# Two weights asked for in two pieces each, and a new order of every engine's work

## The chip, the cores and the metric

The kernel runs on one core of a Trainium2 chip. The time is the device time of one execution in microseconds. Before the change the median of three runs is 166.47 us (165.52 to 167.43). The profile is of one further execution, recorded by the hardware profiler, with its own time.

## The reference

Two stages, one behind the other. The first is a linear attention with a decay and a bonus (RWKV-5), for 4 batches, 8 heads, 768 steps and a head size of 48:

```
for t in range(S):
    kt, vt, rt = (k[:, :, t], v[:, :, t], r[:, :, t])
    cur = np.einsum('bhd,bhe->bhde', u[None] * kt, vt)
    y[:, :, t] = np.einsum('bhd,bhde->bhe', rt, state + cur)
    state = w[None, :, :, None] * state + np.einsum('bhd,bhe->bhde', kt, vt)
```

The second is an MLP mixer on x, the heads of y side by side (4 x 768 x 384):

```
xt = x.transpose(0, 2, 1)
h = np.maximum(xt @ w_tok1, 0.0) @ w_tok2       # 768 -> 256 -> 768, along the tokens
u = x + h.transpose(0, 2, 1)
h2 = np.maximum(u @ w_ch1, 0.0) @ w_ch2         # 384 -> 1536 -> 384, along the channels
return (u + h2).astype(np.float32)
```

## The kernel before, in words

**Units.** The sequence of each batch is cut into 6 chunks of 128 steps, so there are 24 units, numbered 0 to 23; unit u belongs to batch u // 6. For each unit SP loads three tiles k, r and v (128 x 384 f32, 192 KB each; `load`, L742). `kp` and `rp` multiply k and r by powers of the decay, on VectorE or POOL. `trk` and `trr` transpose them on TensorE (from unit 14 on a DMA does), `rk` copies them out, `at` makes the scores inside the chunk, `AT` masks them (for some halves `raw` copies first), `vb` casts v on ScalarE, `kv` adds k times v to the running state in PSUM, `S` copies the state out, `pg` and `yd` make the bonus term, `yS` and `y` add up the unit's output, and `x` writes it as bf16. Unit 3 adds its bonus by a matmul in f32 (`yi3`).

**Mixer.** When the six x of a batch are there, `hid` (six pairs of matmuls with w_tok1) makes the hidden layer of the tokens, `hr` the relu, and `bk` (or `ux` and `ub`, for the first half of batch 0, directly transposed) multiplies by w_tok2. `us` adds x, `tu` and `uT` transpose, `z` makes the channels' hidden layer in 12 pieces of 128 (j = 0 to 11) for each half of the batch, `zr` its relu, `h` the product with w_ch2 in four quarters, `os` adds u, and SP stores.

**Weights.** POOL asks for the weights by DMA, cast to bf16 on the way (`weight`, L753): w0 is w_tok1, w1 is w_tok2, w2 and w4 are the two halves of w_ch1, w3 and w5 those of w_ch2. Each stands in POOL's queue between products; the queue is served in order.

**What sets the order.** Each engine's work is written out by name in `ORDER` (L508). `graph` (L181) builds all steps with what they wait for and with costs; `Plan.run` replays `ORDER` with these costs, and the program is emitted in the order of the starts found. The costs and the `wafter` table (after which step a weight is asked for) shape only this replay, that is, how the engines' instructions are interleaved in the program and where `fill` puts small idle matmuls (27 of them before, all ahead of the first `z`). On the chip each engine takes its own instructions in order, and waits are on what an instruction reads or overwrites. The load of k of unit 6 is held until y5 is done, so that weights go first. SP, at most eight loads in flight, issues loads in `ORDER`'s succession.

All instructions go through one helper, so the profile has them under its line, L617; tiles tell them apart: `ld_k`, `ld_r`, `ld_v` the loads, `kpr` the products, `tr_ps` the transposes, `at_ps` the scores, `y_ps` the output, `h_ps` both `hid` and `h`, `z_ps` the channels' hidden layer, `hT_ps` and `ut_ps` the product with w_tok2, `wtok` and `wch` the weights, `osb` the result.

Of the kernel before, what the change touches and what calls it, by code (L numbers as in the profile page):

```python
# [21 lines left out]
B, H, S, D = 4, 8, 768, 48  # L22
T = 128
C = S // T
G = C // 2
HP = H // 2
NJ = 12
# [146 lines left out]
MM = 0.165  # L174
# [6 lines left out]
def graph(do, cfg):  # L181
# [39 lines left out]
    def weight(i, after):  # L221
        wi[i] = s = p.add(f"i:w{i}", [("POOL", 0.9, cfg.get("wseen", 1.0), True)], after, rank=-50, emit=do("weight", i))
        took = cfg.get("wtime", (3.0, 2.6, 3.1, 7.7, 3.1) if 5 not in cfg["wafter"] else (3.0, 2.6, 3.1, 3.9, 3.1, 3.9))[i]
        wx[i] = p.transfer(f"x:w{i}", s, took, took + 1.0, -1.0)
# [123 lines left out]
    for b in range(B):  # L348
# [20 lines left out]
        for sg in range(2):  # L369
            if (b, sg) in direct:  # L370
                last = C * (b + 1) - 1
                for mm in range(3):
# [4 lines left out]
                    t = p.add(f"ub{n}", [("PE", 2 * MM + 0.01, 2 * MM + 0.14)], [t, wx[1]] + (hr if mm else first), rank=r - 0.2 + 0.01 * mm, emit=do("ub", b, sg, mm))  # L377
# [5 lines left out]
            for c in range(sg * G, sg * G + G):  # L383
                n = 3 if (b, c) in cfg.get("xpe", ()) else 2
                bk = p.add(f"bk{b}_{c}", [("PE", n * MM + 0.01 * (b > 0), n * MM + 0.13 + 0.01 * (b > 0))], hr + [wx[1]], take=True, rank=r + 0.01 * c, emit=do("bk", b, c))
# [10 lines left out]
        for sg in range(2):  # L396
            zr = []
            for j in range(NJ):
                old = downs[2 * b + sg - 3] if 2 * b + sg >= 3 else []
                if j == 0:  # L400
                    z0, z_before = None, z0
                z = p.add(f"z{b}_{sg}_{j}", [("PE", 3 * MM, 3 * MM + 0.13)], [z_before if j == 0 else z0] + old + uT[3 * sg:3 * sg + 3] + [wx[2] if j < NJ // 2 else wx[4]], take=True, rank=m + 0.1 * sg + 0.001 * j, emit=do("z", b, sg, j))
                z0 = z if j == 0 else z0
                ways = [ACT1, DVEP + (False, 0.3)] if b in cfg.get("zr_dve", range(B)) else [ACT1]
                zr.append(p.add(f"zr{b}_{sg}_{j}", ways, [z], give=[f"z{b}_{sg}_{j}"], rank=o, emit=do("zr", b, sg, j)))
            downs.append([])
            for si in range(3):
# [3 lines left out]
                for part in range(parts):  # L411
                    h, n, mm = None, f"{b}_{c}" + "ab"[part] * (parts > 1), MM / parts + (0.005 if parts > 1 else 0.0)
                    for q in range(4):
                        x = 3 * mm + (own if q == 0 else 0.0)
                        h = p.add(f"h{n}_{q}", [("PE", x, x + 0.13)], zr[3 * q:3 * q + 3] + [wx[3] if q < 2 else wx.get(5, wx[3]), h], take=(q == 0), rank=m + 0.1 * sg + 0.05 + 0.01 * si + 0.001 * part - (0.02 if q else 0), emit=do("h", b, c, q, part, parts))
# [22 lines left out]
    for s in p.steps:  # L438
# [41 lines left out]
    + [('w', 0), ('w', 1), ('w', 2), ('w', 4), ('w', 3), ('w', 5)],  # L480
    wafter={0: 'x:r4', 1: 'kp5', 2: 'rp5', 4: 'rp5', 3: 'rp5', 5: 'rp5'},
    slack={'v5': 0.9},
# [4 lines left out]
    wtime=(3.0, 2.6, 3.1, 5.2, 3.1, 3.9),  # L487
# [13 lines left out]
    half=8.3,  # L501
# [41 lines left out]
    ),  # L543
    "ACT": (
# [558 lines left out]
```

## Time and profile before

| | us |
|---|---|
| median of three runs | 166.47 |
| the profiled execution | 165.6 |
| its span, from the first to the last instruction | 163.9 |
| TensorE busy | 154.8 |
| VectorE busy | 119.7 |
| ScalarE busy | 74.0 |
| POOL busy | 59.1 |

The page shows busy time by engine, 40 slices of the span (a digit is the busy share in tenths), and the chain of work that ended last, followed back from the end. Matmuls overlap in the array, so the busy time of TensorE is not work at its peak. A row of the timeline has start, length, engine, line, operation, output<-inputs and count, and in brackets the idle time before it with what ended it. A row of the stretches has the busy time and count of each engine in its window, then the granted clock of TensorE, the share of the DMA engines and GB/s. A landing is counted from the start of the issuing instruction.

### The profile page before, as it was taken

What the parts mean: (1) busy time and instruction counts of PE and PEld (TensorE: products, weight loads), DVE (VectorE), ACT (ScalarE), POOL (GpSimd) and SP (SyncE); (2) the same over time, 40 slices, a digit from 0 to 9 for tenths busy, and PEclk for the clock granted to TensorE, in tenths of its full rate; (3) what the DMA queues carried; (4) which work ended last, traced back from release to release, by engine and by line L of the source; (5) the groups of instructions that cost most, each with busy time, mean ns of one, the idle gap of its engine ahead of it and who ended that gap; (6) DMA issues with size and microseconds to landing.
All of it is one profiled execution on the core that took longest, in us unless ns stands there. A gap on an engine that the chain in (4) does not pass through costs nothing.

```text
span 163.9 us, 3809 instructions
## 1 busy us (share of the span) xinstructions
PE 154.8 (94%) x1487; PEld 99.2 (61%) x1487; DVE 119.7 (73%) x254; ACT 74.0 (45%) x160; POOL 59.1 (36%) x74
## 2 busy tenths in 40 slices
PE   6988799999999999999999999999999999999990
PEld 3476565656576767665666565666566666655670
DVE  5679878547089998896998989999999665223330
ACT  4899671552389635588504420445134102621400
POOL 7157860000055495954459542182702000000000
PEclk9999789999999999999999999999999999999997
DMA  5999999999999998999499999999934032501212
GB/s 106 222 212 219 152 201 201 185 184 198 199 221 237 210 233 168 214 159 208 99 167 206 226 212 150 236 234 151 204 67 145 0 72 43 177 0 48 96 48 98
DMA packets 97427, 26.26 MB, mean 160 GB/s; under 512 B 90753, under 2 KB 97410, under 8 KB 97410
## 3 DMA queue, kind: packets, MB, share of 16 engines
q1 hardware_dynamic: 93920, 22.88, 69.9%
q0 software_dynamic: 3488, 3.15, 12.1%
q8 instruction: 11, 0.18, 0.4%
q14 instruction: 6, 0.05, 0.1%
q10 hardware_dynamic: 2, 0.00, 0.0%
HBM read 20.65 MB, written 4.72 MB: 155 GB/s over the span
## 4 chain that ended last, share of the span: by engine, by line
PE 84%; SPq 7%; DMA 3%; ACT 3%; issue 1%; DVE 0%; ACTq 0%
PE h_ps L617 34%; PE z_ps L617 29%; SPq L617 7%; PE y_ps L617 6%; PE at_ps L617 5%; PE hT_ps L617 4%; DMA ld_v<-in_v_dram 3%; PE tr_ps L617 3%; PE kv_ps L617 3%; ACT rk L617 1%; PE t_ps L617 1%; ACT raw L617 0%; ACT vb L617 0%; PE ut_ps L617 0%; ACT S L617 0%
## 5 line engine op out<-in xcount | busy, mean ns | idle before, releaser
L617 PE MATMUL h_ps<-wch,zr 128*128 128x384 bf16 (+1 forms) x300 | 55.2, 320 | 0.0
L617 PE MATMUL z_ps<-uT,wch 128*128 128x384 bf16 x288 | 53.9, 326 | 0.1
L617 ACT ACTIVATE zr<-z_ps 128x384 bf16<-128x384 f32 x66 | 30.8, 492 | 50.7 <-PE z_ps L617 50.2
L617 PEld LDWEIGHTS <-zr 128*128 128x128 bf16 x300 | 27.4, 98 | 15.2
L617 PEld LDWEIGHTS <-wch 128*128 128x128 bf16 x288 | 26.6, 98 | 16.2 <-issue 0.2
L617 DVE TENSOR_TENSOR AT<-at_ps,mask 128x512 bf16<-128x512 f32 x43 | 28.9, 684 | 1.5 <-PE at_ps L617 1.2
L617 DVE TENSOR_SCALAR zr<-z_ps 128x384 bf16<-128x384 f32 x30 | 15.9, 553 | 11.7 <-PE z_ps L617 11.2
L617 POOL TENSOR_TENSOR kpr<-ld_r,wp 128x384 bf16<-128x384 f32 x14 | 14.6, 1044 | 24.9 <-DVE pr L617 22.2
L617 POOL TENSOR_TENSOR kpr<-ld_k,wn 128x384 bf16<-128x384 f32 x16 | 16.3, 1019 | 10.0 <-DMA ld_k<-in_k_dram 5.8
L617 DVE TENSOR_TENSOR osb<-u_sb,h_ps 128x384 f32<-128x384 bf16 (+1 forms) x22 | 11.7, 532 | 11.0 <-PE h_ps L617 11.0
L617 ACT COPY rk<-tr_ps 128x512 bf16<-128x512 bf16 (+1 forms) x23 | 15.1, 682 | 8.9 <-PE tr_ps L617 8.8
L617 PEld LDWEIGHTS <-rk 48*128 48x128 bf16 (+1 forms) x272 | 11.0, 97 | 8.7 <-issue 4.6
L617 PEld LDWEIGHTS <-kpr 128*128 128x128 bf16 x192 | 12.5, 101 | 5.2 <-issue 1.6
L617 POOL TENSOR_TENSOR yd<-vb,adg 128x384 f32<-128x384 bf16 x12 | 10.3, 858 | 12.0 <-ACT vb L617 8.3
L617 DVE TENSOR_TENSOR x_b<-y_ps,yd 128x384 bf16<-128x384 f32 x23 | 12.6, 552 | 2.1 <-PE y_ps L617 1.9
L617 ACT CAST vb<-ld_v 128x384 bf16<-128x384 f32 x24 | 12.2, 514 | 3.4 <-DMA ld_v<-in_v_dram 3.3
L617 DVE TENSOR_TENSOR u_sb<-x_b,hT_ps 128x384 bf16<-128x384 bf16 x21 | 11.2, 549 | 2.3 <-PE hT_ps L617 1.9
L617 PE MATMUL tr_ps<-ident,kpr 128*128 128x128 bf16 x112 | 10.7, 233 | 1.0 <-ACT rk L617 0.6
L617 PEld LDWEIGHTS <-wtok 128*128 128x128 bf16 x90 | 8.1, 97 | 4.8 <-issue 0.4
L617 PE MATMUL at_ps<-rk 48*128 48x128 bf16 x192 | 9.8, 222 | 1.2 <-ACT rk L617 0.4
L617 DVE TENSOR_TENSOR pr<-tr_ps,rk 128x512 bf16<-128x512 bf16 x14 | 5.9, 419 | 5.9 <-ACT rk L617 5.8
L617 PE MATMUL h_ps<-x_b,wtok 128*128 128x384 bf16 x48 | 10.0, 325 | 0.0
(87 smaller groups left out, 157.5 us busy)
## 6 DMA issues: line engine op xcount, KB each, us to landing
ld_k<-in_k_dram SPq DMA_DIRECT2D x24, 192.0 KB, 3.8
ld_r<-in_r_dram SPq DMA_DIRECT2D x24, 192.0 KB, 3.9
ld_v<-in_v_dram SPq DMA_DIRECT2D x24, 192.0 KB, 3.8
out_dram<-osb SPq DMA_DIRECT2D x23, 192.0 KB, 2.3
wch<-in_moe_w_ch_dram POOLq DMA_DIRECT2D x4, 576.0 KB, 12.2
wtok<-in_moe_w_tok_dram POOLq DMA_DIRECT2D x2, 384.0 KB, 5.4
u_bc<-in_u_dram SPq DMA_DIRECT2D x1, 192.0 KB, 4.4
out_dram<-osb SPq DMA_DIRECT2D x2, 96.0 KB, 2.6
```

The lines of the kernel that those rows point to most:

```text
L617: ins = tc.keep_in_program_order(f(*args, **kw))
```

## The change

Three things. w1 is split by columns into w1 (the first 384) and w6 (the others), w2 into w2 (the first 256 columns, j = 0 and 1) and w7 (the next 512, j = 2 to 5), so there are eight weight transfers in place of six; products wait for the piece that they read. In the planner w0 is asked for after the transfer of v of unit 4 in place of r of unit 4, w1 and w2 after that of r of unit 5, and the times of the transfers are other numbers. And the order of all five engines is new.

```diff
-                    t = p.add(f"ub{n}", [("PE", 2 * MM + 0.01, 2 * MM + 0.14)], [t, wx[1]] + (hr if mm else first), rank=r - 0.2 + 0.01 * mm, emit=do("ub", b, sg, mm))
+                    t = p.add(f"ub{n}", [("PE", 2 * MM + 0.01, 2 * MM + 0.14)], [t, wx[1 if sg == 0 else 6]] + (hr if mm else first), rank=r - 0.2 + 0.01 * mm, emit=do("ub", b, sg, mm))
...
-    + [('w', 0), ('w', 1), ('w', 2), ('w', 4), ('w', 3), ('w', 5)],
-    wafter={0: 'x:r4', 1: 'kp5', 2: 'rp5', 4: 'rp5', 3: 'rp5', 5: 'rp5'},
-    slack={'v5': 0.9},
+    + [('w', 0), ('w', 1), ('w', 2), ('w', 6), ('w', 7), ('w', 4), ('w', 3), ('w', 5)],
+    wafter={0: 'x:v4', 1: 'x:r5', 2: 'x:r5', 6: 'rp5', 7: 'rp5', 4: 'rp5', 3: 'rp5', 5: 'rp5'},
+    slack={'v5': 0.6},
...
-    wtime=(3.0, 2.6, 3.1, 5.2, 3.1, 3.9),
+    wtime={0: 3.0, 1: 1.4, 2: 1.15, 6: 1.4, 7: 2.1, 3: 5.2, 4: 3.1, 5: 3.9},
...
-    half=8.3,
+    half=9.0,
...
-        t, src = [(wtok1, moe_w_tok1), (wtok2, moe_w_tok2), (wch1, moe_w_ch1), (wch2, moe_w_ch2), (wch1, moe_w_ch1), (wch2, moe_w_ch2)][i]
-        cols = {2: slice(0, dch // 2), 4: slice(dch // 2, dch)}.get(i, slice(None))
-        rows = {3: slice(0, NJ // 2), 5: slice(NJ // 2, NJ)}.get(i, slice(None)) if 5 in CFG["wafter"] else slice(None)
+        t, src, rows, cols = {
+            0: (wtok1, moe_w_tok1, slice(None), slice(None)),
+            1: (wtok2, moe_w_tok2, slice(None), slice(0, G * T)),
+            6: (wtok2, moe_w_tok2, slice(None), slice(G * T, S)),
+            2: (wch1, moe_w_ch1, slice(None), slice(0, 2 * 128)),
+            7: (wch1, moe_w_ch1, slice(None), slice(2 * 128, dch // 2)),
+            4: (wch1, moe_w_ch1, slice(None), slice(dch // 2, dch)),
+            3: (wch2, moe_w_ch2, slice(0, NJ // 2), slice(None)),
+            5: (wch2, moe_w_ch2, slice(NJ // 2, NJ), slice(None)),
+        }[i]
```

The head of the new order, as far as it is spoken of below (before, then after):

```diff
 SP
-i:k1 i:r2 i:k0 i:r0 i:r1 i:v0 i:k2 i:v1 i:k3 i:r3 i:v2 i:k4 i:r4 i:k5 i:v3 i:r5 i:v4 i:v5 i:k6 i:r6 i:k7 i:r7 i:v6
+i:r0 i:k1 i:k0 i:k2 i:r1 i:r2 i:r3 i:v0 i:k3 i:v1 i:v2 i:r4 i:k4 i:v4 i:v6 i:k5 i:r5 i:v5 i:v3 i:r6 i:k6 i:r7 i:k7
 POOL
-kp2 kp3 rp3 kp4 rp4 i:w0 kp5 rp5 i:w1 i:w2 i:w4 i:w3 i:w5 rp8
+rp1 kp3 rp3 kp4 rp4 i:w0 kp5 i:w1 rp5 i:w2 i:w6 i:w7 i:w4 i:w3 i:w5 kp6 kp7 rp8
 ACT
-vb2 rk3 wGm vb3 rk4 S3 vb4 rk5 x3 S4 raw5 vb5 hr0_1a
+wGm S1 vb2 rk3 rk4 vb4 vb3 S3 rk5 vb5 x3 raw5 S4 hr0_0a
 DVE
-S2 yd2 AT1_3 pr4 yd3 AT1_4 AT0_4 x2 pr5 AT0_5 AT1_5 yd5 yd4 x4 x5 hr0_0a
+S2 yd2 pr3 AT1_3 AT0_3 pr4 AT1_4 yd3 x2 AT0_4 yd4 pr5 AT0_5 yd5 AT1_5 x4 x5 hr0_1a
 PE
-trk4 at3 pg3 trr4 kv3 y2 trk5 at4 yS3 trr5 yi3 y3 kv4 pg4 at5 yS5 pg5 ux0_0_1 yS4 y4 y5 hid0_0 hid0_1 hid0_2 hid0_3 hid0_4 hid0_5 ux0_0_2
+trk4 yS2 y2 trr4 at3 trk5 at4 pg4 pg3 yS3 kv3 trr5 yi3 kv4 y3 at5 yS4 y4 pg5 hid0_0 hid0_1 hid0_2 yS5 y5 hid0_3 hid0_4 ux0_0_0 hid0_5 ux0_0_1
```

The program after has 40 of the idle matmuls in place of 27; its other matmuls are the same. In the whole order, DVE has 230 steps in place of 237, ScalarE 150 in place of 152, POOL 69 in place of 58.

More of the change, by code (lines that the diff above doesn't have):

```diff
@@ L222, in weight @@
         wi[i] = s = p.add(f"i:w{i}", [("POOL", 0.9, cfg.get("wseen", 1.0), True)], after, rank=-50, emit=do("weight", i))
-        took = cfg.get("wtime", (3.0, 2.6, 3.1, 7.7, 3.1) if 5 not in cfg["wafter"] else (3.0, 2.6, 3.1, 3.9, 3.1, 3.9))[i]
+        took = cfg["wtime"][i]
         wx[i] = p.transfer(f"x:w{i}", s, took, took + 1.0, -1.0)
@@ L384, in graph @@
                 n = 3 if (b, c) in cfg.get("xpe", ()) else 2
-                bk = p.add(f"bk{b}_{c}", [("PE", n * MM + 0.01 * (b > 0), n * MM + 0.13 + 0.01 * (b > 0))], hr + [wx[1]], take=True, rank=r + 0.01 * c, emit=do("bk", b, c))
+                bk = p.add(f"bk{b}_{c}", [("PE", n * MM + 0.01 * (b > 0), n * MM + 0.13 + 0.01 * (b > 0))], hr + [wx[1 if c < G else 6]], take=True, rank=r + 0.01 * c, emit=do("bk", b, c))
                 us = p.add(f"us{b}_{c}", [ACT1, DVEP] if n == 3 else [DVEP], [bk], give=[f"bk{b}_{c}"], rank=r, emit=do("us", b, c))
@@ L401, in graph @@
                     z0, z_before = None, z0
-                z = p.add(f"z{b}_{sg}_{j}", [("PE", 3 * MM, 3 * MM + 0.13)], [z_before if j == 0 else z0] + old + uT[3 * sg:3 * sg + 3] + [wx[2] if j < NJ // 2 else wx[4]], take=True, rank=m + 0.1 * sg + 0.001 * j, emit=do("z", b, sg, j))
+                z = p.add(f"z{b}_{sg}_{j}", [("PE", 3 * MM, 3 * MM + 0.13)], [z_before if j == 0 else z0] + old + uT[3 * sg:3 * sg + 3] + [wx[2 if j < 2 else 7 if j < NJ // 2 else 4]], take=True, rank=m + 0.1 * sg + 0.001 * j, emit=do("z", b, sg, j))
                 z0 = z if j == 0 else z0
@@ L414, in graph @@
                         x = 3 * mm + (own if q == 0 else 0.0)
-                        h = p.add(f"h{n}_{q}", [("PE", x, x + 0.13)], zr[3 * q:3 * q + 3] + [wx[3] if q < 2 else wx.get(5, wx[3]), h], take=(q == 0), rank=m + 0.1 * sg + 0.05 + 0.01 * si + 0.001 * part - (0.02 if q else 0), emit=do("h", b, c, q, part, parts))
+                        h = p.add(f"h{n}_{q}", [("PE", x, x + 0.13)], zr[3 * q:3 * q + 3] + [wx[3 if q < 2 else 5], h], take=(q == 0), rank=m + 0.1 * sg + 0.05 + 0.01 * si + 0.001 * part - (0.02 if q else 0), emit=do("h", b, c, q, part, parts))
                     ways = [ACT1, DVEP] if (b, sg) in direct else [DVEP]
@@ L531 @@
     "DVE": (
[11 rows of a table removed]
[11 rows of a table added]
     ),
     "ACT": (
[8 rows of a table removed]
[8 rows of a table added]
     ),
     "POOL": (
-        "kp2 kp3 rp3 kp4 rp4 i:w0 kp5 rp5 i:w1 i:w2 i:w4 i:w3 i:w5 rp8 kp8 kp9 kp10 yd7 yd8 rp11 yd9 rp12 kp12 yd10 yd11 rp13 kp13 yd12 "
-        "kp14 rp14 rp16 ku14 ku15 ku16 kp16 yd14 rku16 yd16 ku18 rku18 yd15 kp19 rp18 kp18 rp19 yd17 rku19 kp20 rp21 rku20 rp22 kp21 yd19 "
-        "kp23 ku23 rku22 rp23 yd23 "
[3 rows of a table added]
     ),
     "SP": (
[5 rows of a table removed]
[5 rows of a table added]
         "i:o3_3 i:o3_4 i:o3_5a i:o3_5b "
```

89 rows, old and new, of the table ORDER are left out of this document.

## The prediction

> **What bounds the kernel now.** I read the page first, then the chain in order of time, the stretches, and the head's timeline engine by engine.
>
> ```profile
> span 163.9 us, 3809 instructions
> PE 154.8 (94%) x1487; PEld 99.2 (61%) x1487; DVE 119.7 (73%) x254; ACT 74.0 (45%) x160; POOL 59.1 (36%) x74
> PE   6988799999999999999999999999999999999990
> PEclk9999789999999999999999999999999999999997
> PE 84%; SPq 7%; DMA 3%; ACT 3%; issue 1%; DVE 0%; ACTq 0%
> 29.88:42.74 12.86, 12.86 (x88) 8.00 (x88) 6.36 (x14) 4.88 (x10) 0.00 (x0) 1.00 1.15 187
> 42.74:155.00 112.26, 111.62 (x1072) 70.74 (x1071) 88.73 (x178) 48.54 (x107) 43.45 (x45) 1.00 0.78 157
> ```
>
> The columns after the length are TensorE, weight loads, VectorE, ScalarE and POOL, then the clock. TensorE is dense: from 29.88 to 42.74 us it is never idle, from 42.74 to 155 for 112.26 - 111.62 = 0.64 us. Its digits below 9 lie in the first five slices of 4.1 us. What is left to win or lose lies there; a start of the dense part that moves by some time moves the end by the same, because no stall behind it is large enough to take it up. There the chain runs through the loads:
>
> ```profile
> 12.83 4.69 DMA ld_v<-in_v_dram
> 17.54 0.51 ACT vb L617
> 18.05 0.92 ACT rk L617
> ...
> 24.23 0.57 PE y_ps L617 x20
> 24.80 2.19 PE h_ps L617 x12
> ```
>
> The load that lands at 17.52 is v of unit 3, the 15th that SP asks for. Units 4 and 5 hang behind it, then the six hidden products of batch 0 (hid0), whose last pair starts at about 26.5:
>
> ```profile
> 24.64 2.34 PE L617 MATMUL h_ps<-x_b,wtok 128*128 128x384 bf16 x12
> 27.21 0.50 PE L617 MATMUL at_ps<-wtok,h1r 128*128 128x384 bf16 x2
> 29.88 1.14 PE L617 MATMUL z_ps<-uT,wch 128*128 128x384 bf16 x6
> ```
>
> (26.98 is the end of the group; two matmuls pass from the start of the last pair, 0.16 and 0.33 us.)
>
> **The change part by part.** *Weights in two pieces.* Two more issues on POOL; the weights' issues take 0.77 to 0.89 us.
>
> ```profile
> 13.79 1.00 POOL L617 TENSOR_TENSOR kpr<-ld_k,wn 128x384 bf16<-128x384 f32 x1 [0.81 <-DMA ld_k<-in_k_dram]
> 14.90 1.00 POOL L617 TENSOR_TENSOR kpr<-ld_r,wp 128x384 bf16<-128x384 f32 x1
> 15.85 0.89 POOL L617 DMA_DIRECT2D wtok<-in_moe_w_tok_dram  x1
> 19.25 0.77 POOL L617 DMA_DIRECT2D wtok<-in_moe_w_tok_dram  x1
> 20.02 3.19 POOL L617 DMA_DIRECT2D wch<-in_moe_w_ch_dram  x4
> DMA to landing us min/median/max: 5.2/5.2/5.2
> DMA to landing us min/median/max: 8.3/8.3/8.3
> ```
>
> The second token weight lands at 19.25 + 5.2 = 24.4 and is first read at 27.2; the first up weight lands at 20.02 + 8.3 = 28.3 and is read at 29.88. Neither ends a wait that the chain shows, so having their first halves earlier is worth 0 us while hid0 comes no earlier than now. The 1.6 us of POOL push rp5 back by one issue (0.8); trr5, its reader, stands behind kv3 on TensorE and waits longer for that anyway (below). If the cover were gone, it would cost that 0.8. The Trainium skill ("DMA: Bandwidth & Descriptors", section on the anatomy of one DMA on the GpSimd path) gives each such DMA a fixed 2.0 us, which speaks against pieces: two more would, as an estimate from the page, be 4 us if nothing hid them. No landing here decides it, but four issues 0.8 us apart kept the queue full, so I do not count it.
>
> *First weight behind v of unit 4.* In the program no wait for v4 stands on it: `i:w0` follows `rp4` on POOL, before and after. What moves it is k4, which SP now asks for as 13th load, not 12th. Loads go out at (16.51 - 0.81) / 17 = 0.92 us each (first and 18th issue, rows below), so kp4, rp4 and w0 come about 0.9 to 1.0 later: w0 at 16.8.
>
> *The new succession of loads* decides the case. SP now asks in the order ... r4 k4 v4 v6 k5 r5 v5 v3 r6: v3 goes from 15th to 19th, with v of unit 6, whose products on TensorE stand behind trk6 (40 us), ahead of it. The 18th load before is v5:
>
> ```profile
> 0.81 0.45 SPq L617 DMA_DIRECT2D ld_k<-in_k_dram  x1
> ...
> L617 SPq DMA_DIRECT2D ld_v<-in_v_dram x2: 937/1368/1798, 14.7 to 16.5; - x2
> ...
> DMA to landing us min/median/max: 5.0/5.3/5.7
> ...
> DMA to landing us min/median/max: 3.3/3.9/5.9
> ...
> q0 software_dynamic: 525, 0.27, 134.1%
> q1 hardware_dynamic: 30, 0.00, 2.3%
> ```
>
> The first two rows are v4's and v5's issue (ns, shortest to longest; v5 at 16.51) and landing, the third is that of all v loads up to 60 us. v5 took 5.7 us against 3.9 in the median, landing at 22.2. The last two rows (18.75 to 20.25 us) say why: w0's packets had the engines almost to themselves. After the change one more load and w0 still stand ahead of v3, and w0 moves by the same 0.9 to 1.0 as v3's issue, so v3 meets w0 as v5 did: V = 22.2 + 0.92 = 23.1. Were w0 not later at all, the same 19 loads and w0 would still have to pass: again 23.1. Bounds: 19.9 (no contention) and 23.9 (w1's first piece beside it too, half of its 1.6 us).
>
> *What waits for V.* On TensorE kv3 stands ahead of trr5, yi3, kv4, y3, at5, yS4, y4 and hid0; on ScalarE vb3 ahead of S3, rk5, vb5, x3, raw5 and S4; on VectorE yd3 ahead of x2, AT0_4, yd4 and pr5. All this piles up behind one load and is then run off in order, mostly at ScalarE's pace:
>
> ```profile
> 18.86 0.63 ACT L617 CAST S<-kv_ps 48x192 bf16<-48x192 f32 x2
> 20.52 1.01 ACT L617 COPY rk<-tr_ps 128x1024 bf16<-128x1024 bf16 x1 [0.35 <-PE tr_ps L617]
> 22.23 0.48 ACT L617 CAST x_b<-y_ps 128x384 bf16<-128x384 f32 x1 [0.69 <-PE y_ps L617]
> 23.27 0.58 ACT L617 CAST raw<-at_ps 128x512 bf16<-128x512 f32 x1
> 18.27 0.36 PE L617 MATMUL y_ps<-vb,AT 128*128 128x48 bf16 x8
> 23.29 0.33 PE L617 MATMUL y_ps<-S,rk 128*128 128x96 bf16 x4
> L617 DVE TENSOR_TENSOR x_b<-y_ps,yd 128x384 bf16<-128x384 f32 x23 | 12.6, 552 | 2.1 <-PE y_ps L617 1.9
> ```
>
> From V: vb3 0.53, kv3 0.4, S3 0.63, rk5 1.0, vb5 0.5, x3 0.5, raw5 0.6, S4 0.6 make 4.75; yS5 and y5 0.55; x5 0.55; then hid0_5, the last pair, at V + 5.9 = 29.0. hid0_0 to hid0_2 and hid0_4 lie beside it; TensorE has nothing else, as its queue is in order.
>
> *The clock.* The trace shows a stretch at half clock:
>
> ```profile
> 15.28:18.69 3.41, 2.20 (x41) 1.45 (x38) 3.14 (x7) 2.42 (x6) 2.84 (x4) 1.00 0.85 153
> 18.69:22.10 3.41, 3.29 (x32) 2.10 (x29) 2.98 (x6) 2.32 (x5) 3.41 (x5) 0.50 1.31 197
> 20.28 1.59 PE L617 MATMUL y_ps<-yd,ident_w 128*128 128x384 f32 x2
> ```
>
> A stretch of 3.41 us with 2.20 us of work was followed by one at 0.50, and that one, 3.29 busy, by full clock. After the change TensorE has less than 2 us of work between 19 and 23 (trk5, at4, pg4, pg3, yS3), so half clock should last into the run-off: yi3 takes its 1.59 again (about 0.8 at full clock, an estimate from its half) and hid0_0 to hid0_2, six matmuls of 0.16, twice their 1.0. Between 0 (all hidden by ScalarE) and 1.8 (0.8 and 1.0 in full) I take 0.6, since raw5 and S4 hide part. The Trainium skill ("TensorE: Matmul & The Clock Gate", Part 1) says that the clock falls after at least one idle window of about 3.4 us; the row's window was busy for 64%, so it differs from the page, and I go by the row. By the page the term would be 0, and the sum 0.6 less.
>
> *Everything behind.* The order of units 6 to 23 changes on every engine, trk6 comes nine products earlier, and nine products more stand on POOL (1.0 us each) and seven steps fewer on VectorE (0.55). TensorE's matmuls are the same but for 40 fillers in place of 27, all ahead of hid0. The cover is TensorE's density, with 0.64 us idle in 112: an order can win at most that 0.64, and one late tile costs about as much (-0.6 to +1.0; I take 0, between them). k6 is held until y5, which comes 3 us later than now, and it took long to land beside the weights:
>
> ```profile
> DMA to landing us min/median/max: 10.7/10.7/10.7
> ```
>
> Asked for at 28.5 it would land at 39.2, and kp6 be done at 40.3 on POOL; trk6, behind 16 products of 0.49 us, stands at about 33 + 8 = 41, so it is just in time.
>
> *Sum.* hid0_5 at 23.1 + 5.9 + 0.6 = 29.6 instead of 26.5: +3.1; three products of ux0 now stand ahead of it, -0.2. So +2.9. The profiled execution took 165.6 us (span 163.9 and 1.7 around it): 168.5. The median of the runs shown is 166.47, 0.9 above it; 169.4 from there. I take 169.0, between.
>
> **The rivals.** *v3 slips in ahead of w0* (no change). The issue of the 17th load took 1.80 us before, twice the usual, and only thereby came v5 behind w0. Without that, v3 is asked for 0.9 us sooner, at 16.6, and lands 3.9 later at 20.5, its warm run-off ends at 26.4, less 0.2: 165.6 - 0.3 = 165.3, or 165.8 between the two frames. Against it: w0 is only one load's time later. *The same and the clock kept* (the other side: faster). If v3 lands by 19.9 (16.6 and 3.3, the shortest of the v loads), TensorE's pause is too short to lose the clock, hid0_5 comes at 25.8, and the later 0.64 of stalls goes too: -0.7 - 0.2 - 0.6 = -1.5, 164.1, or 164.6. It decides from V = 20.2 on downwards. For it: the stretch at half clock, which makes yi3 alone take 1.59 where about 0.8 would do. Against it: v6 takes 0.92 us ahead of v3. *Half clock reaches into the dense part* (slower still). Stretches of 3.41 us end at 25.5, 28.9 and 32.3; if the run-off doesn't fill the one up to 28.9, the 2.7 us from 29.6 to 32.3 do half their work, +1.4: 170.4. *The change does not do what it says*: w0 has no wait for v4; this leaves the sum as it is, shown above.
>
> **How the numbers follow.** Forecast (169.0) 0.50, half clock further 0.15, v3 ahead of w0 0.22, and that with the clock kept 0.13. A measurement tells about 1% from no change here: 164.8 to 168.1. So faster 0.13, same 0.22, slower 0.65. The range leaves out most of the faster case and the top of the slowest: 165.3 to 171.0. The forecast's own range is 167.6 to 170.0.
>
> **What would show it.** In the profile after: v3's landing near 23 us, a wait of ScalarE's vb for ld_v of 3 us or more, hardly any TensorE work from 20 to 23, a half clock that lasts beyond 22.1, hid0's last pair near 29.6 and the first z product near 33 (29.88 before), then 130 us to the end of TensorE as before. w0 issued near 16.8. It would be wrong if v3 landed by 21, if vb3's followers ran faster than ScalarE's order lets them, or if TensorE's idle time behind 42 us grew or shrank by more than 1 us.

## The result and the profile after

The changed kernel takes 170.62 us (median of four executions, 169.83 to 170.93) against 166.0 before (median of four): a ratio of 1.031, with an interval of 1.026 to 1.036, so it is slower by about 3%. The profiled execution took 169.83 us with a span of 167.8, against 165.6 and 163.9: +4.2 and +3.9. The forecast was 169.0 us, an increase of 1.5% over the 166.47 us that stood for the kernel before and of 1.8% over 166.0: the direction and the place were right, the size was too small. (A ratio here is of undisturbed executions alone and can differ from the quotient of the medians: single executions of the kernel before scatter from 165.7 to 171.9 us in the experiments' sessions, and a quarter to somewhat over half of those are left out, as are six of ten with v6 behind v3, four of ten with the pieces alone, two of four with whole weights and three of four with whole weights on the same plan.)

The page of the kernel after, the same rows as before; the last is ScalarE's `vb`, with its idle time and what ended it:

```profile
span 167.8 us, 3843 instructions
PE 154.9 (92%) x1500; PEld 99.5 (59%) x1500; DVE 116.6 (70%) x247; ACT 71.8 (43%) x158; POOL 67.9 (40%) x85
PE   6978609999999989999999999999999999999991
PEclk9999956999999999999999999999999999999999
PE 81%; SPq 9%; DMA 4%; ACT 2%; DVE 1%; issue 1%
L617 ACT CAST vb<-ld_v 128x384 bf16<-128x384 f32 x24 | 12.0, 513 | 5.7 <-DMA ld_v<-in_v_dram 5.7
```

TensorE is busy for as long as before (154.8), so the 3.9 us are idle time, and the digits put it into one slice, the sixth: a 0 between 21.0 and 25.2 us. Behind that slice the row is as dense as it was. All that VectorE and ScalarE were relieved of (3.1 and 2.2 us) does not show in the time.

The chain of work that ended last, after, from the load of v of unit 3 on (start, length, what):

```profile
17.54 6.73 DMA ld_v<-in_v_dram
24.29 0.52 ACT vb L617
24.85 0.48 PE kv_ps L617 x4
25.33 0.43 PE tr_ps L617 x4
25.76 1.39 PE y_ps L617 x2
...
30.99 0.17 PE at_ps L617 x3
31.15 0.33 PE h_ps L617 x2
```

v of unit 3 (v3) lands at 24.27 us instead of 17.52, and from `kv` of unit 3 on every link is TensorE's, up to the last pair of hidden products (hid0_5). By TensorE's timeline that pair starts at 30.99 instead of 26.5; its link in the chain begins only where the link before it ends. The stretches show TensorE's pause, the clock, and the dense part from the first z product to the start of the last matmul (TensorE, weight loads, VectorE, ScalarE, POOL, clock, DMA share, GB/s). After:

```profile
17.83:21.24 3.41, 1.73 (x32) 1.12 (x30) 2.03 (x4) 0.78 (x2) 2.70 (x4) 1.00 1.02 138
21.24:24.65 3.41, 0.00 (x0) 0.00 (x0) 0.00 (x0) 0.36 (x1) 3.41 (x6) 0.50 1.31 205
24.65:28.07 3.42, 3.22 (x28) 2.23 (x29) 2.51 (x5) 2.45 (x6) 1.29 (x2) 0.50 1.33 202
28.07:31.48 3.41, 3.41 (x54) 2.52 (x51) 2.52 (x5) 1.46 (x5) 0.00 (x0) 1.00 1.19 211
24.85:30.99 6.14, 6.14 (x73) 4.39 (x73) 5.01 (x10) 3.63 (x8) 1.09 (x2) 0.74 1.27 207
34.15:164.15 130.00, 129.06 (x1200) 82.41 (x1197) 93.87 (x188) 50.81 (x114) 50.78 (x54) 1.00 0.74 150
```

And the same dense part before:

```profile
29.88:159.67 129.79, 129.15 (x1196) 82.18 (x1196) 96.56 (x195) 53.42 (x117) 43.45 (x45) 1.00 0.79 156
```

The dense part starts 4.27 us later and lasts 130.00 us instead of 129.79. What follows, to the end of the span, is 0.6 us shorter (3.6 us, 4.2 before). 4.27 + 0.21 - 0.6 = 3.9: that is the whole difference of the spans.

Why the load took 6.73 us shows in what the DMA engines moved between its issue and its landing: packets, then by queue (q1 the loads, q0 the weights; the last figure of a row is the share of the engines' time). Before, for v of unit 5, the load on which the forecast was built (16.5 to 22.25 us; the first row has the engines' busy tenths in 40 slices of that window):

```profile
DMA  6200279999559999999999999999999999989899
DMA packets 3183, 0.98 MB, mean 170 GB/s; under 512 B 2316, under 2 KB 3183, under 8 KB 3183
q0 software_dynamic: 883, 0.55, 69.2%
q1 hardware_dynamic: 2300, 0.43, 39.8%
```

After, for v3 (17.55 to 24.3 us):

```profile
DMA packets 4484, 1.17 MB, mean 173 GB/s; under 512 B 3585, under 2 KB 4484, under 8 KB 4484
q1 hardware_dynamic: 3569, 0.68, 63.6%
q0 software_dynamic: 915, 0.49, 51.9%
...
q0 software_dynamic: 582, 0.30, 86.4%
q1 hardware_dynamic: 581, 0.11, 41.6%
```

The rate is the same, 170 and 173 GB/s; what differs is the amount. The weights' packets are about as many, but 1269 more of the loads' passed. Not all of these stood ahead of v3. The loads' packets from the start of the span, up to the landing of v5 before and up to that of v3 after:

```profile
q1 hardware_dynamic: 18720, 3.54, 82.3%
...
q1 hardware_dynamic: 20360, 3.85, 84.1%
```

The first count is 18 loads of 1040 packets and nothing more, as the load behind v5 is the held k6. The second is 19 loads (19760 packets) and 600 packets of a twentieth: r6, which the new succession puts between v3 and the held k6, and which SP asked for at 18.24. So of the 1269 packets about 670, two thirds of a load, stood ahead of v3, and 600 belong to the load behind it and passed beside it. Both queues together moved 0.19 MB more. At 173 GB/s that is 1.1 us, and the landing took 6.73 - 5.72 = 1.01 us longer. How much of it r6 costs is not shown: no run holds back r6 alone.

The last two rows of the view of after are from 19.5 to 22.0 us: weights and loads go packet by packet, 582 to 581. The Trainium skill ("DMA: Bandwidth & Descriptors", the paragraph on arbitration under queues, rings and completion order) says that each DMA engine takes the queues in turn, a packet at a time. Equal counts agree with it; the 525 to 30 of the kernel before, quoted in the prediction, do not look like turns.

### The profile page after: what moved, and what is told of

Its sections match the earlier page's. It is cut to its first block, busy times and chain, and to the rows that moved or that the text cites. A ratio compares the mean times of both kernels' runs of the same rounds, so it can differ in the third digit from the quotient of the medians.

```text
span 167.8 us, 3843 instructions
## 1 busy us (share of the span) xinstructions
PE 154.9 (92%) x1500; PEld 99.5 (59%) x1500; DVE 116.6 (70%) x247; ACT 71.8 (43%) x158; POOL 67.9 (40%) x85
## 4 chain that ended last, share of the span: by engine, by line
PE 81%; SPq 9%; DMA 4%; ACT 2%; DVE 1%; issue 1%
PE h_ps L617 33%; PE z_ps L617 28%; SPq L617 9%; PE y_ps L617 5%; PE at_ps L617 4%; DMA ld_v<-in_v_dram 4%; PE hT_ps L617 3%; PE kv_ps L617 3%; PE tr_ps L617 2%; PE t_ps L617 1%; ACT rk L617 1%; DVE S L617 0%; ACT vb L617 0%; PE ut_ps L617 0%; ACT osb L617 0%
## 5 line engine op out<-in xcount | busy, mean ns | idle before, releaser
L617 ACT ACTIVATE zr<-z_ps 128x384 bf16<-128x384 f32 x65 | 29.9, 490 | 54.4 <-PE z_ps L617 53.7
L617 PEld LDWEIGHTS <-zr 128*128 128x128 bf16 x300 | 27.5, 98 | 15.5
L617 DVE TENSOR_TENSOR AT<-at_ps,mask 128x512 bf16<-128x512 f32 x43 | 28.4, 683 | 4.4 <-PE at_ps L617 4.4
L617 POOL TENSOR_TENSOR kpr<-ld_k,wn 128x384 bf16<-128x384 f32 x17 | 17.1, 1009 | 26.2 <-DMA ld_k<-in_k_dram 19.2
L617 DVE TENSOR_SCALAR zr<-z_ps 128x384 bf16<-128x384 f32 x31 | 16.6, 553 | 8.1 <-PE z_ps L617 7.0
L617 POOL TENSOR_TENSOR yd<-vb,adg 128x384 f32<-128x384 bf16 x16 | 13.2, 829 | 18.6 <-ACT vb L617 7.8
L617 POOL TENSOR_TENSOR kpr<-ld_r,wp 128x384 bf16<-128x384 f32 x15 | 15.9, 1062 | 11.8 <-DVE x_b L617 6.3
L617 DVE TENSOR_TENSOR u_sb<-x_b,hT_ps 128x384 bf16<-128x384 bf16 x21 | 10.7, 549 | 2.9 <-PE hT_ps L617 2.8
L617 PE MATMUL kv_ps<-vb,kpr 128*128 128x96 bf16 x80 | 7.0, 213 | 4.7 <-ACT vb L617 4.7
```

What stands on the lines that cost most here:

```text
L617: ins = tc.keep_in_program_order(f(*args, **kw))
```

## The experiments

Theory A: the place of v3 in SP's succession is the whole cost; all engines wait for it, and nothing behind takes up or adds time. Rivals: the pieces cost time (B), the new order of the other engines costs time (C), the weights' packets, not the place, make v3 late (D), and half clock is the larger part (E).

### v3 early: its place alone undone

The changed kernel with v3 and v6 exchanged in SP's order.

```diff
-i:v2 i:r4 i:k4 i:v4 i:v6 i:k5 i:r5 i:v5 i:v3 i:r6 i:k6
+i:v2 i:r4 i:k4 i:v4 i:v3 i:k5 i:r5 i:v5 i:v6 i:r6 i:k6
```

> The changed kernel with one swap in SP's succession of loads: v3 and v6 change places (r4 k4 v4 v3 k5 r5 v5 v6 r6), nothing else in any engine's order. If the late v3 is what costs (theory): v3 lands at about 17.1 to 17.6 us, where v6 did, the run-off behind it is over before v5 comes, and v5, still landing near 23.6, becomes the last: vb5, x3, raw5, S4, yS5, y5, x5 behind it give hid0's last pair at about 27.0 in place of 31.0; time about 166 us, level with the kernel before (ratio 0.99 to 1.01). If the new order of units 6 to 23 or the pieces of the weights cost (rivals): it stays within 1 us of the changed kernel, 169.5 us or more.

Measured: 166.89 us, a ratio to the kernel before of 1.002 (0.997 to 1.006). Profiled: 166.24 us, span 163.9; v3 lands at 17.64, hid0_5 starts at 25.86, the first z product at 30.27. One row of TensorE's timeline and two stretches, the run-off from `kv` of unit 3 to hid0_5 and the dense part:

```profile
28.48 0.82 PE L617 MATMUL hT_ps<-h1r,wtok 128*128 128x384 bf16 x4 [1.08 <-DMA wtok<-in_moe_w_tok_dram]
20.75:25.86 5.11, 4.86 (x72) 3.46 (x71) 5.05 (x11) 3.43 (x8) 5.11 (x7) 1.00 1.35 209
30.27:160.26 129.99, 129.04 (x1199) 82.45 (x1197) 93.64 (x188) 50.86 (x114) 50.32 (x54) 1.00 0.79 156
```

One exchange of two loads takes the loss away; pieces and the new order of four engines are still in. B and C fall as causes of the loss. The clock stays full. The first row is what then ends last: hid0_5 is 0.6 us earlier than before, but the second piece of the second token weight lands at 28.43 and TensorE waits 1.08 us for it, so the first z product is 0.4 later than before.

### v3 late in the kernel before: its place alone changed

```diff
-i:r4 i:k5 i:v3 i:r5 i:v4 i:v5 i:k6 i:r6 i:k7 i:r7 i:v6 i:r8
+i:r4 i:k5 i:v4 i:v6 i:r5 i:v5 i:v3 i:k6 i:r6 i:k7 i:r7 i:r8
```

> The kernel before with only SP's succession of loads changed: v6 and v5 ahead of v3 (k5 v4 v6 r5 v5 v3), all engines' orders as before, weights whole. If the place of v3 is the cause (theory): v3 lands at about 24 us, kv3, at4 and all behind it start 6 us later than now, hid0's last pair comes at 31 us or later in place of 26.5, and the time is 4 to 6 us above the kernel before (ratio 1.025 to 1.04), as large as the whole change. If the cause lies in the new orders of the engines or the pieces: within 1 us of the kernel before.

Measured: 171.96 us, a ratio of 1.033 (1.025 to 1.041). Its chain around v3, the load packets from v3's issue to its landing (17.85 to 23.2 us), and its dense part:

```profile
15.57 2.24 SPq L617
17.85 5.34 DMA ld_v<-in_v_dram
...
q1 hardware_dynamic: 2236, 0.42, 39.3%
...
35.04:165.49 130.45, 129.25 (x1199) 82.16 (x1197) 98.30 (x195) 53.59 (x118) 43.64 (x45) 1.00 0.75 148
```

The kernel before with nothing new but v3 as its 19th load loses as much as the whole change does. With the experiment above, A stands from both sides. Here v3 lands at 23.19, 1.1 earlier than in the changed kernel; its queue was shorter and the held k6 stands directly behind it, so the 2236 packets are its own and those ahead of it alone. Still the first z product comes at 35.04, 0.9 later: the old order of the other engines runs off behind v3 in 8.75 us (to hid0_5 at 31.94), the new one in 6.72. So in these two profiles the new order of the engines is the better one for a late v3; it wins back some of what the new succession costs.

### v6 behind v3

The changed kernel with v6 moved behind v3, so that v3 is the 18th load, not the 19th.

```diff
-i:v4 i:v6 i:k5 i:r5 i:v5 i:v3 i:r6
+i:v4 i:k5 i:r5 i:v5 i:v3 i:v6 i:r6
```

> The changed kernel with only v6 moved behind v3 (r4 k4 v4 k5 r5 v5 v3 v6 r6), so that one load less stands ahead of v3. By the rate of the head, 0.92 us a load, v3 would land at 23.3 and the time fall by 0.9 us, to 169.7. By the packets of the changed kernel, which take turns one to one with those of the first weight from 19 to 22 us and then flow at double speed, v3 takes the place that v5 had there (23.6 us against 24.3), and the time falls by 0.6 us. If both, v5 and v3, now pass before the first weight's packets come: v3 near 20.5 and 3 to 4 us less.

Measured: 169.93 us median. Four of its executions lie between 166.7 and 169.0, six between 169.6 and 170.9; the ratio, 1.007 (0.999 to 1.015), is of the four. The profiled one is of the first group (167.84 us, span 165.1). Two rows of POOL's timeline in it, and the stretch at half clock:

```profile
16.86 0.99 POOL L617 TENSOR_TENSOR kpr<-ld_k,wn 128x384 bf16<-128x384 f32 x1 [3.28 <-DMA ld_k<-in_k_dram]
...
18.74 0.90 POOL L617 DMA_DIRECT2D wtok<-in_moe_w_tok_dram  x1
...
17.89:21.30 3.41, 3.39 (x40) 3.00 (x41) 1.10 (x2) 1.46 (x3) 3.39 (x4) 0.50 0.92 157
```

k of unit 4 landed late, POOL waited 3.28 us for it, and the first weight was asked for at 18.74 instead of 16.64. v3 slipped in ahead of it and landed at 21.24; the first z product came at 31.44, behind the second token weight, whose second piece landed at 29.6. This is the rival "v3 slips in ahead of w0" of the prediction, met here with one load less. That the other six executions are those in which it does not slip in is likely, but was not seen: none of them was profiled.

### The first weight behind all early products

The changed kernel with `i:w0` behind `rp5` on POOL, so that the loads run without the weights.

```diff
-rp1 kp3 rp3 kp4 rp4 i:w0 kp5 i:w1 rp5 i:w2 i:w6
+rp1 kp3 rp3 kp4 rp4 kp5 rp5 i:w0 i:w1 i:w2 i:w6
```

> The changed kernel with the first weight asked for behind rp5 in POOL's queue, not behind rp4, so that all loads up to v3 pass before its packets. If the first weight's packets beside the loads are why v3 lands at 24.3 and not at 23.1 (theory): v3 lands at 20.5 to 21.5, the run-off's ScalarE part ends at about 27; but the first weight then lands at 25.5 to 26.5 and hid0 starts no sooner, so hid0's last pair comes at 27.5 to 28.5 in place of 31.0 and the time falls by 2.5 to 3.5 us, to 167 to 168.5. If the loads themselves or SP's issues set v3's landing: v3 stays at 23 or later and the time does not fall.

Measured: 168.24 us, ratio 1.010 (1.005 to 1.014). v3's link of the chain, what passed until it landed (18.0 to 21.7 us), and the dense part:

```profile
17.95 3.79 DMA ld_v<-in_v_dram
...
DMA packets 3731, 0.71 MB, mean 191 GB/s; under 512 B 3731, under 2 KB 3731, under 8 KB 3731
...
32.51:162.50 129.99, 129.05 (x1200) 82.45 (x1197) 93.92 (x188) 50.81 (x114) 50.80 (x54) 1.00 0.79 155
```

v3 needs 3.79 us instead of 6.73, with as many load packets (3731, and 3569 after): 2.9 us of its landing are the weights' packets. D holds for this part, 2.9 of the 6.75 us that v3 is late after the change. But the kernel is still 1% slower than before: v3 lands at 21.74, four us later than in the kernel before, on its place alone. hid0_5 comes at 29.35, not at 27.5 to 28.5 as expected. hid0 starts at 27.14; the weight had landed at 25.90, and 13 idle matmuls, which the replay put ahead of hid0 in this run, stood before it for 0.7 us.

### The first weight one product later, in the kernel before

```diff
-kp2 kp3 rp3 kp4 rp4 i:w0 kp5 rp5 i:w1
+kp2 kp3 rp3 kp4 rp4 kp5 i:w0 rp5 i:w1
```

> The kernel before with the first weight asked for one product later on POOL, behind kp5 in place of rp4. Its packets then come 1 us later, v5 passes before them and lands near 20 to 21 in place of 22.2; the first weight lands near 22.5, still ahead of hid0's first product (24.6). By the chain, which there runs from v3 (17.5) through ScalarE, the gain is small: 0 to 1 us, ratio 0.994 to 1.0. If it slows: the later weights are what z waits for.

Measured: 166.75 us, ratio 0.997 (0.993 to 1.002). The last v, of unit 5, lands at 20.34 instead of 22.23, and the clock stays full. hid0_5 starts at 25.61, 0.9 earlier than before; the first z product at 29.71, only 0.2 earlier, because the weights, asked for later, are now waited for (0.37 and 0.35 us at their first readers). What the loads win the weights lose. The dense part behind is 131.27 us in this profile, 1.5 longer than before, 1.0 of it one wait of the scores for a transpose by DMA, so the span of 165.0 us is no shorter either.

### Pieces alone, in the kernel before

The kernel before with w1 and w2 in two pieces each and the two new issues on POOL, its orders otherwise its own.

```diff
-kp2 kp3 rp3 kp4 rp4 i:w0 kp5 rp5 i:w1 i:w2 i:w4 i:w3 i:w5
+kp2 kp3 rp3 kp4 rp4 i:w0 kp5 rp5 i:w1 i:w2 i:w6 i:w7 i:w4 i:w3 i:w5
```

> The kernel before with the two weights in pieces (first pieces in the old places, second pieces behind them), the orders and the succession of loads as before. Theory: no piece ends a wait there, as both weights are in before they are read: within 0.7 us of the kernel before (ratio 0.996 to 1.004). If pieces cost by their packets or issues: 1 us or more above. If they help: 1 us below.

Measured: 167.71 us, ratio 0.997 (0.991 to 1.004). The pieces neither cost nor bring anything that this can tell (the interval leaves from -1.5 to +0.7 us): as a cause of over 4 us, B falls.

### Whole weights in the changed kernel, twice

First with the weights whole in the planner too, which replays the order with one transfer for each.

```diff
-rp1 kp3 rp3 kp4 rp4 i:w0 kp5 i:w1 rp5 i:w2 i:w6 i:w7 i:w4 i:w3 i:w5
+rp1 kp3 rp3 kp4 rp4 i:w0 kp5 i:w1 rp5 i:w2 i:w4 i:w3 i:w5
```

> The changed kernel with the second token weight and the first up weight asked for whole again, all else as changed (the first still behind v of unit 4, the order the same). Theory: neither piece ends a wait, and two DMAs less save POOL 1.6 us that nobody waits for: within 0.6 us of the changed kernel (170.6). If the 672 packets more or the issues between kp5 and rp5 cost: 1 us or more below the changed kernel. If the pieces help (first halves earlier): 1 us or more above it.

Measured: 174.72 us, ratio 1.040 (1.031 to 1.048): no faster than the change itself (1.026 to 1.036), as far as two intervals that overlap can tell. Its dense part, and POOL's row for `kp` of units 6 and 7:

```profile
35.45:166.82 131.37, 129.21 (x1199) 82.38 (x1197) 93.62 (x188) 50.86 (x114) 50.09 (x54) 1.00 0.72 147
...
43.83 1.95 POOL L617 TENSOR_TENSOR kpr<-ld_k,wn 128x384 bf16<-128x384 f32 x2 [18.73 <-DVE kpr L617]
```

The replay came out otherwise: `kp` of unit 6 now waits for a product of VectorE, not for its load, starts at 43.83 (40.08 after), and the dense part is 1.4 us longer. So this run compares two plans and says nothing of the pieces. The second one keeps the plan and only makes the transfers whole, in the places of the first pieces:

```diff
+        if i in (6, 7):
+            return
...
-            1: (wtok2, moe_w_tok2, slice(None), slice(0, G * T)),
+            1: (wtok2, moe_w_tok2, slice(None), slice(None)),
...
-            2: (wch1, moe_w_ch1, slice(None), slice(0, 2 * 128)),
+            2: (wch1, moe_w_ch1, slice(None), slice(0, dch // 2)),
```

> The changed kernel with the two weights asked for whole in the places of their first pieces, and every other instruction and wait as in the changed kernel (in the earlier run with whole weights the planner also made kp6 wait for a product of VectorE, and trk6 came 1.2 us late for that alone). Theory: the pieces cost and bring nothing, 169.8 to 171.8 like the changed kernel, 130.0 us from the first z product to the last matmul. If pieces bring something: 1 us or more above that; if they cost: 1 us or more below.

Measured: 171.51 us. Its four executions scatter from 168.72 to 172.5 and give no ratio, so the time decides nothing. Its dense part is 130.00 us (35.60 to 165.60), as after, so the extra 1.4 us of the run before it was the plan's. What pieces are worth rests on the pieces in the kernel before.

### The changed kernel again, and TensorE kept at work

The changed kernel once more, and a version of it with 42 idle matmuls behind `yS3`, in the pause, to keep the clock up.

> The changed kernel as it is, as the level for the runs beside it: 170 to 171 us, ratio 1.025 to 1.036, with v3 landing near 24 us.

Measured: 171.49 us, ratio 1.028 (1.021 to 1.035). Its chain at SP's last loads and v3, the load packets from v3's issue to its landing (18.5 to 25.85 us), the run-off, and the dense part:

```profile
14.41 2.54 SPq L617
17.00 0.61 SPq L617
17.65 0.80 SPq L617
18.49 7.34 DMA ld_v<-in_v_dram
...
q1 hardware_dynamic: 4331, 0.82, 60.9%
...
26.40:32.97 6.57, 6.56 (x73) 4.72 (x73) 5.08 (x10) 3.63 (x8) 1.08 (x2) 0.67 1.25 206
36.13:166.12 129.99, 129.04 (x1199) 82.39 (x1197) 93.86 (x188) 50.81 (x114) 50.80 (x54) 1.00 0.73 148
```

The same kernel, and v3 lands at 25.83, 1.6 us later than in the first profile and 1.8 later than expected; the dense part behind is again the same.

```diff
+            if s.name == "yS3":
+                fill("PE", 42)
```

> The changed kernel with 42 idle matmuls more on TensorE between yS3 and kv3, where it only waits for v3, so that its clock may be full again when the run-off starts. If the half clock costs on the path (theory): the run-off from v3's landing to hid0's last pair takes 5.9 to 6.2 us in place of 6.7, and the time falls by 0.5 to 0.8 us. If ScalarE alone sets the run-off: no difference beyond 0.3 us. If the idle matmuls end after v3 has landed, they cost what they overhang, up to 0.5 us.

Measured: 175.15 us, ratio 1.050 (1.043 to 1.058). TensorE's row for the idle matmuls, and the run-off behind them:

```profile
27.40 3.84 PE L617 MATMUL fill_ps<-idle 128*128 128x128 bf16 x42 [6.09 <-DVE yd L617]
31.25:36.36 5.11, 4.75 (x75) 3.45 (x74) 2.95 (x6) 3.42 (x8) 0.00 (x0) 1.00 1.27 204
```

As a way to fill the pause this missed: the idle matmuls took a PSUM tile that `yd` of unit 3 had to leave first, and that stands behind v3, so they ran behind the pause: `kv` of unit 3 comes 5.0 us behind v3's landing (26.23), not 0.6. But they warmed the clock, and so measured what was in dispute. From `kv` of unit 3 to hid0_5 it takes 5.11 us at clock 1.00, as it does with v3 early; 6.14 at 0.74 after; 6.57 at 0.67 in the run above. The two at full clock differ in what the other engines had left to do (VectorE is busy for 2.95 us in one, 5.05 in the other) and still take the same time, so the difference to 6.14 and 6.57 is put down to the clock: half clock costs 1.0 to 1.5 us. E is true for that much, about a quarter of what the first z product is late (1.0 of 4.27, 1.5 of 6.25 us). The larger part is the landing: v3 comes 6.75 us later than before, and the new order gives 2.3 of that back by a shorter run-off (6.72 us from the landing to hid0_5, 8.98 before).

### Two attempts to go below the kernel before

v3 early, and the second piece of the token weight (w6) ahead of the up weight's first (w2), for the wait of 1.08 us seen above:

```diff
-rp4 i:w0 kp5 i:w1 rp5 i:w2 i:w6 i:w7
+rp4 i:w0 kp5 i:w1 rp5 i:w6 i:w2 i:w7
...
-i:v4 i:v6 i:k5 i:r5 i:v5 i:v3 i:r6
+i:v4 i:v3 i:k5 i:r5 i:v5 i:v6 i:r6
```

> The changed kernel with v3 and v6 changed places, as in the run with v3 early, and besides the second piece of the second token weight asked for ahead of the first piece of the up weight. In the run with v3 early TensorE waited 1.2 us for that second piece (28.4 us) ahead of the first hT product. It should land 1.0 to 1.2 us sooner, at about 27.3, the first z product come at 29.3 in place of 30.3, and the time fall by about 1 us below that run: ratio to the kernel before 0.990 to 0.998. If the first up piece, now last, becomes the wait (28.4, z wants it at 29.2): still 0.8 won.

Measured: 166.8 us, ratio 0.998 (0.994 to 1.002). TensorE still waits for the second token weight, and now for the up weight as well:

```profile
28.99 0.82 PE L617 MATMUL hT_ps<-h1r,wtok 128*128 128x384 bf16 x4 [0.48 <-DMA wtok<-in_moe_w_tok_dram]
...
32.16 1.15 PE L617 MATMUL z_ps<-uT,wch 128*128 128x384 bf16 x6 [0.56 <-DMA wch<-in_moe_w_ch_dram]
```

The expected gain of 1 us did not come. In this profile r of unit 5 landed at 20.81 (19.97 with v3 early alone), POOL waited for it, and the second piece was asked for at 21.89, hardly sooner than with v3 early alone (21.99). It landed at 28.94 and not at 27.3, and the up weight's first piece, now behind it, ended last. The last attempt took v6's 192 KB out of the stream: v6 behind the held k6, and `vb` of unit 6 later on ScalarE.

```diff
-i:v4 i:v3 i:k5 i:r5 i:v5 i:v6 i:r6 i:k6 i:r7
+i:v4 i:v3 i:k5 i:r5 i:v5 i:r6 i:k6 i:v6 i:r7
...
-hr0_0a hr0_0b vb6 uT0_0_1
+hr0_0a hr0_0b uT0_0_1
...
-rkk6 rkr6 os0_0
+rkk6 rkr6 vb6 os0_0
```

> As the run with v3 early and the second token piece ahead of the up piece, and besides v6 asked for behind the held k6, its cast behind rkr6 on ScalarE. One load less (0.92 us) stands among the weights' packets, so the pieces that hT and z waited for there (28.94 and 32.1) come 0.5 to 0.9 us sooner: the time falls by as much below that run, ratio to the kernel before 0.990 to 0.997. If v6 now comes late for kv6: kv6 and h behind it wait, and it is slower than that run.

Measured: 167.12 us, ratio 1.000 (0.995 to 1.004). Its dense part:

```profile
29.18:160.76 131.58, 129.37 (x1199) 82.39 (x1197) 94.20 (x188) 51.34 (x115) 49.86 (x54) 1.00 0.79 156
42.20 0.33 PE L617 MATMUL kv_ps<-vb,kpr 128*128 128x96 bf16 x4 [0.98 <-ACT vb L617]
```

The first z product starts 1.1 us earlier than with v3 early alone (30.27), and the dense part takes 1.6 longer than there, 0.98 of it at `kv` of unit 6, which waits for the late v6. Here a stage behind the head did give a gain back. No version beats the kernel before.

## Why the prediction was right in direction and short in size

**What bounds the kernel: right.** A start of the dense part that moves moves the end by the same: from the first z product to the start of the last matmul 129.79 us before, 130.00 after, and 129.99 with v3 early and with the first weight late. It does not hold of itself in every order: in five of the other runs the stretch takes 130.45 to 131.58 us, and in two of these a late tile is shown above.

**Pieces at 0: right**, by the pieces alone in the kernel before (0.997, with an interval across 1). **w0 at 16.8: right** (16.64). **k6 just in time: right**; it landed at 39.94 and trk6 ran at 42.19, both as forecast to within 1.2 us, without a wait. **Everything behind at 0: right** (+0.2; the 0.6 us that the end of the span is shorter stood in no term). **-0.2 for the three products of ux0: right**; from hid0_5 to the first z product it takes 3.16 us instead of 3.38.

**V, v3's landing: 23.1 forecast, 24.27 measured, and this is the step that failed.** The sum was v5's landing before plus one issue's time: "the same 19 loads and w0 would still have to pass: again 23.1". v3 was issued at 17.54, 1.03 after v5's 16.51, about as taken (0.92). But its landing was taken to last as long as v5's 5.7, and it lasted 6.73, above the bound of 23.9 for V, because more load packets passed until it landed, 3569 against 2300 for v5: two thirds of a load more stood ahead of it, and 600 packets of r6 passed beside it, so that the "19 loads" were 19.6. An issue's spacing was used as if it were a load's price in a queue that weights share; the added bytes make 1.1 us at 173 GB/s, beside the later issue. The rows to see it by were there before: SP's issue of 1.80 us stood directly ahead of v5, and the engines ran nearly empty there (the tenths 6200279 at the start of the window above), so v5 met a short queue; and behind v5 stood the held k6, where the new succession has r6. After the change the long issue (1.99 us) was that of r5, two loads ahead of v3.

**The run-off, 5.9 at ScalarE's pace and 0.6 for the clock: 6.72 measured, by two errors that nearly cancel.** The sign, half clock beyond 22.1, came (to 28.07). But the run-off is not ScalarE's: in the 6.14 us from 24.85 to 30.99 TensorE is busy for all of it and ScalarE for 3.63, and at full clock TensorE is busy for 4.86 of 5.11. So warm it is 24.27 to 24.85 and 5.11, or 5.7, not 5.9; and half clock, which does not hide behind ScalarE, costs 1.0, not 0.6 (inside the bounds of 0 and 1.8).

**The account.** Forecast +2.9; V +1.17, clock +0.43, warm run-off -0.2: +4.3, and measured 4.27 at the first z product. V is the largest error. The forecast in time, 169.0, stood between 168.5 for a profiled execution and 169.4 for the median; these came out at 169.83 and 170.62.

**The rivals.** "v3 ahead of w0" did not happen in the changed kernel, but was seen once with v3 a load earlier. "Half clock further" did not come: the clock is full from 28.07 on, and the dense part starts at 34.15. "That and the clock kept", the faster case, needed V below 20.2: with v3 early V was 17.64 and the clock full, and hid0_5 came at 25.86 (25.8 in the rival). The kernel was level with before all the same, not 1.5 us faster: the second token weight then ended last and held TensorE up for 1.08 us, a wait that the rival had left out, and the 0.64 us of later stalls did not go (129.99 us).

**The page on the clock.** The Trainium skill ("TensorE: Matmul & The Clock Gate", Part 1) gives an idle window of about 3.4 us as what lowers the clock, by which the prediction put the term at 0. The rows of after start half clock at 21.24, behind a stretch that was busy for 1.73 of 3.41 us, and go on with it for one more stretch behind one with no work at all. The first differs from the page, as the row of before did, and there the measurement decides. The second agrees with it, and this is the stretch that cost time, since in the first TensorE had no work: with v3 as late as it was, the page too gives half clock in the run-off.

## What to carry to other kernels

Before a load is moved in a succession, find out who waits for it and what stands behind that waiter in order on every engine: one load of 192 KB moved from 15th to 19th place cost this kernel 3%, and everything else in a change of five orders did not show beside it. Price a place in a shared queue by the bytes that pass until the load has landed, at the measured rate, not by the spacing of the issues: those ahead of it, and part of a load behind it that nothing holds. And look for where a slow issue lets that queue run empty. Where a stage with no slack follows, a gain ahead of it counts only if the next thing that it needs (here the second weight) comes earlier too.

## What was not expected of the hardware

One issue among SP's 16th to 18th loads takes 1.6 to 2.5 us in these profiles, where most of the others take 0.6 to 1.3, and at varying places. With it goes how much still had to pass from the issue of the awaited load to its landing. In load packets, its own 1040 included and those of r6 left out: with the slow issue directly ahead of it 2290 (v5 before, 1.80 us) and 2236 (v3 in the kernel before with v3 late, 2.24 us); two loads ahead 2975 (after, 1.99 us) and 3084 (the first weight late, 2.16 us); three ahead 3372 (the changed kernel again, 2.54 us, where v3 took 7.34 us to land). What makes the issue slow, no run here shows.
